# V's weights split by three engines, and dense products in the first cycle with scores

## The chip, the cores and the metric

The kernel runs on one core of one Trainium2 chip. The metric is the device time of one execution in microseconds (us). A shorter time is better.

## What is computed

The reference is a transformer block with two branches on the same normalised input, summed with the input itself. With `x` of 2048 rows and 512 columns, 32 heads of 16, all in float32:

```python
xn = layernorm(x)
# branch A: attention without a mask
q, k, v = split_heads(xn @ wqkv)            # 32 heads, 16 wide
p = softmax(q @ k.T * 16 ** -0.5)           # 2048 x 2048 for each head
A = merge_heads(p @ v) @ wo
# branch B: a gated MLP with a product over the sequence
z = gelu(xn @ w_in)                          # 2 x 896 columns
z1, z2 = z[:, :896], layernorm(z[:, 896:])
g = w_sp @ z2 + b_sp[:, None]                # 2048 x 2048 times 2048 x 896
B = (z1 * g) @ w_out
out = x + A + B
```

## The kernel before

**Arithmetic.** Every dense product (Q, K, V, both halves of `w_in`, the product over the sequence, `w_out`, `wo`) is made from operands that are split into a high and a low part of type fp32r. The helper `mm3` (lines 169 to 172) issues three matmuls for one product: high by high (L170), low by high (L171) and high by low (L172). In `v_tile` the first operand of `mm3` is the normalised and transposed `x` (`xnT`) and the second is V's weights. So L170 needs the two high parts, L171 the low part of `xnT`, and L172 the low part of the weights.

**The prologue.** Loads of `x` and of the four pieces `wv0` to `wv3` of V's weights are issued in order by SyncE. While they arrive, TensorE makes 15 matmuls on a tile of zeros (L842). A weight piece becomes a high part by a cast (L857, on GpSimd, POOL in the profile) and a low part by a subtraction in `end` (L191, on VectorE, DVE in the profile, for pieces 0 to 2, and on GpSimd for piece 3). The first two tiles of `x` are normalised (`norm_x`, statistics on DVE, L259 to L264; application on ScalarE, ACT in the profile, L268), transposed by TensorE (`turn_x`, L276), and split by `split`: the high part on ACT (L58), the low part on DVE (L167). All engines keep the order in which their instructions are written. In that order DVE makes the three low parts of the weights ahead of the low parts of `xnT`. Then follow `v_tile(0)` and `v_tile(1)`, the other two tiles of the first group of `x`, `v_tile(2)`, and so on through four groups of rows, with the first Q and K.

**The main loop.** Attention runs over 16 pairs of heads, 4 chunks of queries and 16 tiles of keys: 1024 steps. Each step has one tile of scores `st` (two matmuls, L955) whose exponential ACT takes (`exp`, tile `pf`), and, 27 steps ahead, one tile `mx` of scores (L650) of which DVE takes the largest (L658). The `st` and `mx` tiles share three pairs of PSUM banks in turn. Products of the exponentials with V (L929) gather in a PSUM bank with the tag `o`. The loop's variable `half` counts half cycles: an even one has the steps `b` and `b + 1`, an odd one the step `b + 2`, with `b = 3 * (half // 2)`. Negative ones, before the first score, only make `mx` tiles.

**Dense products in between.** A queue of generators (`qk_rest` for the remaining Q and K, then the two halves of `w_in`, the product over the sequence, `w_out`, `wo`) yields one dense product at a time. A `credit` decides how many of them follow a half cycle: 650 stands for one product of three matmuls, 512 columns each. Where `b` is negative each half cycle gets 2600, that is four. From `b = 0` on, an odd half cycle adds the share that spreads what is left over the steps up to `DENSE = 931`, and an even one gets none:

```python
if b < 0:
    credit = 2600
elif half % 2:
    credit = min(credit + 3 * (max(todo / max(DENSE - b, 10), ...
else:
    continue
```

**The accumulators of dense products.** They use the PSUM bank with the tag `d`. The group `qk_group` (four products for Q or for K of 512 rows) may also use V's bank `o` as long as no product with V is under way: while `now[0] < -2` (`now[0]` is the half cycle) its Q goes to `d` and its K to `o`. After the last product of a group, ACT copies the bank to SBUF (`qr`), behind the exponentials that stand ahead of it.

Of the kernel before, what the change touches and what calls it, by code (L numbers as in the profile page):

```python
# [10 lines left out]
AF = mybir.ActivationFunctionType  # L11
# [29 lines left out]
def fused_block(ctx, tc, x, wqkv, wo, w_in, w_spT, b_sp, w_out, out):  # L41
    nc = tc.nc
# [13 lines left out]
    def act(out, in_, func, n, **kw):  # L56
        load["A"] += 0.16 + n / 1400.0
        return nc.scalar.activation(out, in_, func, **kw)  # L58
# [48 lines left out]
    now = [-2 * LEAD // 3 - 1]  # L107
# [8 lines left out]
    def gps(us):  # L116
        pool[0] = max(pool[0], clock()) + us
        return nc.gpsimd
# [28 lines left out]
    def t512(nm):  # L147
        return big.tile([P, 512], F32, tag="t512", name=nm, bufs=4)
# [4 lines left out]
    def dpsum(nm, tag="d", n=1):  # L153
        left[0] = n
        return ps.tile([P, 512], F32, tag=tag, name=nm, bufs=1)
# [13 lines left out]
    def mm3(acc, lh, ll, rh, rl, first, last):  # L169
        nc.tensor.matmul(acc, lh, rh, start=first, stop=False)  # L170
        nc.tensor.matmul(acc, ll, rh, start=False, stop=False)  # L171
        nc.tensor.matmul(acc, lh, rl, start=False, stop=last)  # L172
# [15 lines left out]
    def end(loaded, low=None, high=False):  # L188
        t, rw, n = loaded
        if high:  # L190
            low.tensor_sub(t[:, 1, :n], rw[:, :n], t[:, 0, :n].bitcast(F32))  # L191
        elif low:
            nc.scalar.activation(t[:, 0, :n], rw[:, :n], AF.Copy)
            low.tensor_sub(t[:, 1, :n], rw[:, :n], t[:, 0, :n].bitcast(F32))
        else:
            gps(0.6).tensor_copy(t[:, 0, :n], rw[:, :n])  # L196
            gps(1.3).tensor_sub(t[:, 1, :n], rw[:, :n], t[:, 0, :n].bitcast(F32))  # L197
        return t
# [47 lines left out]
    def norm_x(g, parts=1):  # L246


        mv = sm.tile([P, 4, 2], F32, tag="mv", name=f"mv{g}", bufs=2)
        rs = sm.tile([P, 2, 4], F32, tag="rs", name=f"rs{g}", bufs=2)  # L250
        k = 4 // parts
        for a in range(parts):
            tiles = range(a * k, (a + 1) * k)
            if a:
                yield
            sl = slice(a * k, (a + 1) * k)
            for i in tiles:
                st = sm.tile([P, 6], F32, tag="bst", name=f"bst{g}_{i}", bufs=4)
                nc.vector.bn_stats(st, xs[g, i])  # L259
                nc.vector.bn_aggr(mv[:, i, :], st)  # L260
            yield
            nc.scalar.activation(rs[:, 0, sl], mv[:, sl, 1], AF.Sqrt, bias=epst)
            nc.vector.reciprocal(rs[:, 0, sl], rs[:, 0, sl])
            nc.vector.scalar_tensor_tensor(rs[:, 1, sl], mv[:, sl, 0], -1.0, rs[:, 0, sl], ALU.mult, ALU.mult)  # L264
            for i in tiles:
                if i % 4 == 2:
                    yield
                nc.scalar.activation(xs[g, i], xs[g, i], AF.Identity, bias=rs[:, 1, i:i + 1], scale=rs[:, 0, i:i + 1])  # L268
# [31 lines left out]

    def qk_group(m, g, w, tags=("d",)):
        for a in range(2):
            if now[0] < -2 and m:
                tags = ("d", "o")
            acc = dpsum(f"qk{m}_{a}_{g}", tags[a % len(tags)], ND)
            for c in range(ND):
                t = xnT[g, c]
                mm3(acc, w[a][:, 0, c * P:(c + 1) * P], w[a][:, 1, c * P:(c + 1) * P], t[:, 0, :], t[:, 1, :], c == 0, c == ND - 1)
                yield 650 + 0.5 * (c == ND - 1)
            if m == 0:  # L310
                run(qk_split(m, g, a, acc))
                yield 0
                continue
            raw_ = t512(f"qr{m}_{a}_{g}")
            act(raw_, acc, AF.Copy, 512)
            side.append(qk_split(m, g, a, raw_))
            yield 0

    def qk_split(m, g, a, src):
        hl = hilo(f"qkhl{m}_{a}_{g}")  # L320

        act(hl[:, a, :], src, AF.Copy, 512)
        yield
        if m:
            gps(1.3).tensor_sub(hl[:, 1 - a, :], src, hl[:, a, :].bitcast(F32))  # L325
            yield from pool_done()
        else:
            dve(512).tensor_sub(hl[:, 1 - a, :], src, hl[:, a, :].bitcast(F32))
        (store if m else move)((qscr, kscr)[a][m][:, :, g * 512:(g + 1) * 512], hl)
        yield  # L330
# [483 lines left out]
    def last_add(t, acc):  # L814
        f = fin[t // 2]
        dve(1024).tensor_add(f, acc, f)
        move(out[t * P:(t + 2) * P, :].rearrange("(a p) d -> p a d", p=P), f)
# [5 lines left out]
    def run(gen):  # L823
        for _ in gen:
            pass
# [9 lines left out]
    with tc.manual_schedule(engines=engines):  # L835
# [10 lines left out]
        wv = []  # L846
        for c in range(ND):
            t = (qst, kst)[c // 2][1].rearrange("p (b a f) -> p b a f", b=2, a=2)[:, c % 2]
# [4 lines left out]
        run(load_x(2))  # L853
        ones = big.tile([P, 512], F32, tag="raw", name="ones", bufs=3)
        nc.vector.memset(ones[0:32, 0:P], 1.0)
        for t, rw, n in wv:
            nc.gpsimd.tensor_copy(t[:, 0, :], rw)  # L857
        norm = norm_x(0, 2)
        next(norm)
        next(norm)  # L860
        wv = [end(l, (nc.vector, nc.gpsimd)[c == 3], True) for c, l in enumerate(wv)]
        turn_x(0, 0, 2)
        next(norm)
        nc.gpsimd.dma_start(cscr.rearrange("o (a b) -> (o a) b", b=P), ones[0:16, 0:P])
# [130 lines left out]
        for half in range(-2 * LEAD // 3, 2 * (N // 3 + 4)):  # L995
            b = 3 * (half // 2)
            ms = [b + LEAD] if half % 2 == 0 else [b + LEAD + 1, b + LEAD + 2]
            ns = [n for n in ([b, b + 1] if half % 2 == 0 else [b + 2]) if 0 <= n < N]
            now[0] = half
            flush()  # L1000
            for n in ns:
                if n == 16:
                    init_rows(1)
                if n % 64 == 14 and n // 64 + 1 < NP:
                    load_stacks(n // 64 + 1)
            pause = max(0, pause - 1.5)
            final = []
            if b + LEAD >= NSTEP and half % 2 and turn and turn[0][0] + 1 in added:
                final.append(last_mm(*turn.pop(0)))
            tiles = [(scores, n) for n in ns]  # L1010
            for i, m in enumerate(ms):
                tiles.insert(1 if half % 2 == 0 else 2 * i, (max_mm, m))
            for make, n in tiles:
                make(n)
            while ended:
                chunk_out(*ended.pop(0))
            for n in ns[:1]:
                exp(n)
            if half % 2 == 0:
                pv_some(b - 1, ready // 2 * 2)  # L1020
            for n in ns[1:]:
                exp(n)
            while behind and behind[0][0] <= half:
                nc.scalar.dma_start(*behind.pop(0)[1:])
            for f in final:
                last_add(*f)
            low = min(load.values())
            for e in load:
                load[e] = min(load[e] - low, 2.0)
            limit = load["D"] + (2.5 if half % 2 == 0 else 3.0)  # L1030
            for m in ms:
                max_red(m)

            if half % 2 == 0:
                for m in range(ms[0] - 2, ms[0] + 1):
                    max_fin(m)
            if drain:
                drain = False
                cost = next(queue[0], None)
                if cost is None:  # L1040
                    queue.pop(0)
                else:
                    pause = -cost
            bg[:] = [g for g in bg if next(g, 0) is None]
            side[:] = [g for g in side if load["D"] > limit or next(g, 0) is None]
            ready += len(ns)
            if b < 0:
                credit = 2600
            elif half % 2:
                credit = min(credit + 3 * (max(todo / max(DENSE - b, 10), 600 if b > DENSE - 15 else 0) if todo > 0 else max((todo + 64 * 650) / max(N - 6 - b, 8), 450)), 3250)  # L1050
            else:
                continue
            if urgent and between and not drain and "ones" in sel:
                queue.insert(0, urgent.pop(0))
                pause = 0
            took = 0
            while queue and not pause and not drain and go():
                cost = next(queue[0], None)
                if cost is None:
                    queue.pop(0)  # L1060
                elif cost <= 0:
                    pause = -cost
                else:
                    drain = between = cost % 1 > 0
                    credit -= cost
                    todo -= cost
                    left[0] -= 1
                    took += 1
# [38 lines left out]
```

## Time and profile before

| What | us |
|---|---|
| median of 3 runs (lowest, highest) | 1957.76 (1957.56, 1959.02) |
| the profiled execution, device time | 1960.21 |
| its span, first to last instruction | 1958.4 |
| TensorE busy in the span (matmuls) | 1938.7 |
| VectorE, ScalarE, GpSimd busy | 1373.7, 1232.5, 725.5 |
| mean granted TensorE clock | 0.997 of full |

The span is what the profile covers, and 1.8 us of the device time lie around it. The profiled execution is 2.45 us above the median of the other runs. Times in the profile's rows are counted from the start of the span. A matmul of 512 columns that follows another one starts about 0.23 us after it at the full clock, and the duration in its own row (0.39 us) includes the part in which it overlaps its neighbours.

### The profile page before, as it was taken

How to read it: one execution, taken by the hardware profiler on the slowest of the kernel's cores; microseconds unless marked ns; L12 is line 12 of the kernel's file. 1: busy time of each engine (PE TensorE's matmuls, PEld its weight loads, DVE VectorE, ACT ScalarE, POOL GpSimd, SP SyncE). 2: the span in 40 equal slices, each digit the busy share in tenths (PEclk: the TensorE clock that was granted, in tenths of full speed). 3: DMA queues.
4: the chain of work that ended last, by engine and by line, in shares of the span. 5: the costliest groups of instructions: out<-in, count | busy, mean ns of one | idle time of the engine just before them, and what ended most of it. 6: DMA issues, size and time to landing. Idle time of an engine off the chain costs nothing.

```text
span 1958.4 us, 32641 instructions
## 1 busy us (share of the span) xinstructions
PE 1938.7 (99%) x12559; PEld 1049.7 (54%) x12559; DVE 1373.7 (70%) x1565; ACT 1232.5 (63%) x1407; POOL 725.5 (37%) x790
## 2 busy tenths in 40 slices
PE   8999999999999999999999999999999999999998
PEld 7765555555555555555555555555555555555543
DVE  5356777777767677777777767777777777777872
ACT  4347778888677666656566656665666655556664
POOL 3334278889776931026122531017112400002100
PEclk9999999999999999999999999999999999999999
DMA  7566344363535535365545745346454645355323
GB/s 260 201 219 183 104 120 117 111 179 107 144 132 153 183 117 141 101 166 156 142 137 162 202 131 134 104 120 205 110 158 144 180 140 137 106 147 160 105 73 113
DMA packets 229202, 284.23 MB, mean 145 GB/s; under 512 B 35176, under 2 KB 134136, under 8 KB 226168
## 3 DMA queue, kind: packets, MB, share of 16 engines
q1 hardware_dynamic: 217240, 272.64, 47.9%
q0 software_dynamic: 2592, 8.46, 1.1%
q10 hardware_dynamic: 9216, 1.05, 0.4%
q8 instruction: 99, 1.62, 0.3%
q14 instruction: 55, 0.45, 0.1%
HBM read 188.51 MB, written 93.58 MB: 144 GB/s over the span
## 4 chain that ended last, share of the span: by engine, by line
PE 95%; DVE 2%; ACT 1%; issue 1%; DMA 0%; POOL 0%; SPq 0%; DVEq 0%; ACTq 0%
PE o L929 23%; PE mx L650 16%; PE st L955 15%; PE sp L170 7%; PE sp L172 5%; PE sp L171 5%; PE mo L170 2%; PE qk L170 2%; PE z1p L170 2%; PE z2p L170 2%; PE qk L171 1%; PE qk L172 1%; PE mo L171 1%; PE mo L172 1%; PE z1p L172 1%; PE z1p L171 1%
## 5 line engine op out<-in xcount | busy, mean ns | idle before, releaser
L658 DVE TENSOR_REDUCE mm<-mx 128x2 f32<-128x1024 f32 x1024 | 1221.9, 1222 | 498.2 <-PE mx L650 493.9
L58 ACT ACTIVATE pf<-st 128x1024 f32<-128x1024 f32 x1024 | 1028.8, 1025 | 620.0 <-PE st L955 591.6
L929 PE MATMUL o<-pf,vall 128*32 128x512 f32 (+1 forms) x5120 | 511.0, 513 | 0.0
L650 PE MATMUL mx<-kst,qst 48*128 48x512 f32 x2048 | 446.7, 434 | 2.7 <-ACT pf L58 1.8
L955 PE MATMUL st<-qst,kst 50*128 50x512 f32 x2048 | 445.2, 431 | 1.3 <-DVE mm L658 1.1
L650 PEld LDWEIGHTS mx<-kst,qst 48*128 48x128 f32 x2048 | 192.0, 185 | 268.4 <-ACT pf L58 169.6
L955 PEld LDWEIGHTS st<-qst,kst 50*128 50x128 f32 x2048 | 193.1, 185 | 164.0 <-issue 85.7
L929 PEld LDWEIGHTS o<-pf,vall 128*32 128x32 f32 x5120 | 131.4, 109 | 233.5 <-issue 211.5
L170 PE MATMUL sp<-wsp,zs 128*128 128x512 f32 x448 | 193.9, 433 | 0.3 <-DVE z1i L566 0.2
L573 POOL TENSOR_TENSOR z1i<-z1i,hhl 128x512 f32<-128x512 f32 x28 | 36.0, 1287 | 416.1 <-DVE z1i L566 413.3
L172 PE MATMUL sp<-wsp,zs 128*128 128x512 f32 x448 | 176.0, 393 | 0.0
L171 PE MATMUL sp<-wsp,zs 128*128 128x512 f32 x448 | 176.0, 393 | 0.0
L170 PEld LDWEIGHTS sp<-wsp,zs 128*128 128x128 f32 x448 | 83.9, 187 | 68.9 <-issue 51.8
L172 PEld LDWEIGHTS sp<-wsp,zs 128*128 128x128 f32 x448 | 84.1, 188 | 19.9 <-POOL wsp L197 0.5
L171 PEld LDWEIGHTS sp<-wsp,zs 128*128 128x128 f32 x448 | 84.4, 188 | 12.2
L196 POOL CAST wo<-wo0r 128x512 fp32r<-128x512 f32 x1 | 0.6, 612 | 189.6 <-DMA wo0r<-in_wo 189.6
L325 POOL TENSOR_TENSOR qkhl<-qr,qkhl 128x512 fp32r<-128x512 f32 x24 | 30.9, 1289 | 72.1 <-ACT qkhl L58 72.1
L170 PE MATMUL z2p<-w,xt 128*128 128x448 f32 x128 | 51.3, 401 | 0.0
L170 PE MATMUL mo<-wout,hp 128*128 128x512 f32 x112 | 48.5, 433 | 0.6 <-DVE xr L610 0.4
L711 POOL TENSOR_TENSOR ob<-ob 128x512 f32<-128x512 f32 (+1 forms) x16 | 20.6, 1287 | 72.8 <-DMA ob<-rscr 65.7
L172 PE MATMUL z2p<-w,xt 128*128 128x448 f32 x128 | 46.8, 366 | 0.0
L171 PE MATMUL z2p<-w,xt 128*128 128x448 f32 x128 | 46.7, 365 | 0.0
(382 smaller groups left out, 1986.3 us busy)
## 6 DMA issues: line engine op xcount, KB each, us to landing
zs<-z2scr SPq DMA_DIRECT2D x112, 512.0 KB
escr<-e SPq DMA_DIRECT2D x60, 256.0 KB
hscr<-hhl SPq DMA_DIRECT2D x28, 512.0 KB
xscr<-xnT POOLq DMA_DIRECT2D x16, 512.0 KB, 4.8
qscr<-qkhl SPq DMA_DIRECT2D x16, 512.0 KB
kscr<-qkhl SPq DMA_DIRECT2D x16, 512.0 KB
xt<-xscr SPq DMA_DIRECT2D x64, 128.0 KB
z2scr<-z2hl SPq DMA_DIRECT2D x32, 256.0 KB
```

The costliest lines, as they stand in the source:

```text
L58: return nc.scalar.activation(out, in_, func, **kw)
L170: nc.tensor.matmul(acc, lh, rh, start=first, stop=False)
L171: nc.tensor.matmul(acc, ll, rh, start=False, stop=False)
L172: nc.tensor.matmul(acc, lh, rl, start=False, stop=last)
L196: gps(0.6).tensor_copy(t[:, 0, :n], rw[:, :n])
L325: gps(1.3).tensor_sub(hl[:, 1 - a, :], src, hl[:, a, :].bitcast(F32))
L573: gps(1.3).tensor_add(z1, z1, hl[:, 1, :].bitcast(F32))
L650: nc.tensor.matmul(acc[:, j, :], qst[p % 2][rows, tt * P:(tt + 1) * P], kst[p % 2][rows, kc * 512:(kc + 1) * 512], start=True, stop=True)
L658: dve(1024).tensor_reduce(mmax[i // 16][:, :, t, kc], mstep.pop(i), AX.X, ALU.max)
L711: gps(1.3).tensor_mul(both[rows, 0, :], both[rows, 0, :], both[rows, 2, :])
L929: nc.tensor.matmul(acc[cols:cols + VW, a:a + w], vpack(kt - 1 + r, 2 * p + j), pf[:, j * 512 + a:j * 512 + a + w], start=(kt == 1 and a == ...
L955: nc.tensor.matmul(st[:, j, :], kst[p % 2][rows, kt * P:(kt + 1) * P], qst[p % 2][rows, c * 512:(c + 1) * 512], start=True, stop=True)
```

## The change

It has three parts.

1. **V's weights.** The casts of `wv0`, `wv2` and `wv3` stay on GpSimd and are written after the first part of `norm_x`. The cast of `wv1` goes to ScalarE. The subtraction for `wv2` moves from VectorE to GpSimd, which now makes those of `wv2` and `wv3`; VectorE keeps `wv0` and `wv1`.
2. **The bank of `qk_group`.** Up to half cycle 0, a group takes bank `o` if it is begun in an even half cycle and `d` in an odd one.
3. **The credit.** In the cycle `b = 0`, as long as no product with V has been made, each half cycle gets a credit of 2600, as before the first score. So the even half cycle 0 is followed by dense products too.

```diff
     def qk_group(m, g, w, tags=("d",)):
         for a in range(2):
-            if now[0] < -2 and m:
-                tags = ("d", "o")
+            if now[0] <= 0 and m:
+                tags = ("do"[now[0] % 2 == 0],)
             acc = dpsum(f"qk{m}_{a}_{g}", tags[a % len(tags)], ND)
...
-        for t, rw, n in wv:
-            nc.gpsimd.tensor_copy(t[:, 0, :], rw)
         norm = norm_x(0, 2)
         next(norm)
         next(norm)
-        wv = [end(l, (nc.vector, nc.gpsimd)[c == 3], True) for c, l in enumerate(wv)]
+        for c in (0, 2, 3):
+            nc.gpsimd.tensor_copy(wv[c][0][:, 0, :], wv[c][1])
+        nc.scalar.activation(wv[1][0][:, 0, :], wv[1][1], AF.Copy)
+        wv = [end(l, (nc.vector, nc.gpsimd)[c > 1], True) for c, l in enumerate(wv)]
         turn_x(0, 0, 2)
...
+            before = done
             for make, n in tiles:
                 make(n)
...
             ready += len(ns)
-            if b < 0:
+            if b < 0 or b == 0 and done == before:
                 credit = 2600
```

## The prediction

> **What bounds the kernel now.** I read the page first, then the table of windows, the chain of waits, and the timeline of the stretches that the table pointed to. On the page, engines' busy time and the chain that ended last:
>
> ```profile
> PE 1938.7 (99%) x12559; PEld 1049.7 (54%) x12559; DVE 1373.7 (70%) x1565; ACT 1232.5 (63%) x1407; POOL 725.5 (37%) x790
> ...
> PE 95%; DVE 2%; ACT 1%; issue 1%; DMA 0%; POOL 0%; SPq 0%; DVEq 0%; ACTq 0%
> ```
>
> TensorE (PE) sets the time, and the change removes no matmul: all 12559 stay. Only time in which PE waits, or is fed at a lower clock, can be won. The windows (length, busy time of each engine, then the granted clock) show where:
>
> ```profile
> 10.00:20.00 10.00, 8.42 (x32) 6.50 (x32) 5.44 (x13) 4.16 (x9) 7.11 (x9) 0.83 0.75 270
> 20.00:30.00 10.00, 10.00 (x53) 8.51 (x53) 5.39 (x16) 5.58 (x11) 4.09 (x8) 1.00 0.73 267
> 140.00:160.00 20.00, 19.33 (x119) 10.15 (x118) 13.89 (x17) 14.84 (x19) 3.32 (x4) 1.00 0.36 116
> 1000.00:1500.00 500.00, 499.70 (x3306) 261.95 (x3306) 360.61 (x395) 304.42 (x322) 142.39 (x135) 1.00 0.52 147
> ```
>
> PE idles 1.6 us in 10 to 20, where the clock is also below full, and 0.7 us in 140 to 160, the cycle with the first scores; the long middle has 0.3 us in 500. The chain of waits of the first 60 us (start, length, what):
>
> ```profile
> 7.51 1.10 POOL qst L857
> ...
> 9.63 1.09 DVE kst L191
> 10.72 0.34 DVE xnT L167
> 11.06 0.04 issue
> 11.11 0.50 PE v L171
> ...
> 12.73 0.43 PE v L172
> 13.16 0.43 PE v L170
> ...
> 15.72 0.23 PE v L171
> ```
>
> PE's second product with V waits for the low part of `xnT`, and that stands on DVE behind the low part of `wv2`, whose cast on POOL stands behind that of `wv1`. From 11.88 to 15.25 the products step by 0.43 us instead of 0.23 us. The timeline of the two places:
>
> ```profile
> 8.98 0.47 PE L170 MATMUL v<-qst,xnT 128*128 128x512 f32 x1 [0.56 <-ACT xnT L58]
> 10.26 1.59 POOL L191 TENSOR_TENSOR kst<-wv3r,kst 128x512 fp32r<-128x512 f32 x1
> 10.64 1.40 DVE L167 TENSOR_TENSOR xnT<-xT,xnT 128x256 fp32r<-128x256 f32 x4
> 11.11 0.50 PE L171 MATMUL v<-qst,xnT 128*128 128x512 f32 x1 [1.65 <-DVE xnT L167]
> ...
> 141.00 1.94 ACT L58 ACTIVATE pf<-st 128x1024 f32<-128x1024 f32 x2 [0.59 <-PE st L955]
> 141.01 0.40 PE L955 MATMUL st<-qst,kst 50*128 50x512 f32 x2
> 142.08 0.50 PE L650 MATMUL mx<-kst,qst 48*128 48x512 f32 x2 [0.67 <-ACT pf L58]
> 143.48 0.50 PE L170 MATMUL qk<-xnT__1212,wqk 128*128 128x512 f32 x1
> ```
>
> **The prologue, step by step.** By the landings in the trace `wv0` to `wv3` are there at 6.74, 7.46, 8.10 and 8.74 us.
>
> ACT ends the normalisation of the first two tiles at 7.38. The added cast of `wv1` (0.63, from the row of a 128x512 cast on ACT, `qkhl<-qr`) runs from 7.51 to 8.14. The next thing on ACT, the high part of `xnT`, starts at 8.45 anyway, since it waits for PE's transposes: 0.31 us of cover, so nothing. Were the cast late by more, every microsecond would go to the chain.
>
> DVE: `wv0` from 7.44 to 8.13 as now; `wv1` from 8.20, 1.07 us (its present row, next to a cast on POOL) or 0.69 (the row without a neighbour), so until 9.27 or 8.89; I take the first, because POOL casts `wv2` from 8.15. The low part of `xnT` then starts at 9.25 instead of 10.64, and PE's L171 follows 0.47 behind as now, at 9.72 instead of 11.11: **1.39 us**. Both ends: 1.0 and 1.8.
>
> Clock: the 23 products from this L171 to the end of `v_tile(1)` take 7.11 us now (11.11 to 18.22). At the full step they take 23 x 0.227 = 5.22. So the half clock costs **1.89 us**. The records give it from 11.66 to 15.07, right after a stretch of 3.41 us (8.24 to 11.66) in which PE was 35% busy, transposes counted; at the end of the kernel a stretch with 40% lost the clock too, and the lowest that kept it has 74%. With L171 at 9.72 the first stretch is 76% busy, so I expect the full clock. The Trainium skill, "TensorE: Matmul & The Clock Gate", Part 1, has the same window (3413 ns), two states, and the half rate after an idle window: the trace agrees. By that rule alone, which names no share below which a window is idle, this term is 1.89 too.
>
> POOL: now four casts and the subtraction of `wv3`, ended at 11.85. After: cast `wv0` 6.80 to 7.41; `wv2` from its landing, 8.15 to 8.76; `wv3` 8.77 to 9.84 (1.07, since DVE subtracts); subtraction of `wv2` to 11.14 and of `wv3` to 12.44 (1.29 each, as in the rows of `wqk`; 1.59 next to DVE). PE at full step reaches L172 of the third piece at 11.31, after its low part, and L172 of the fourth at 11.99, before it: **a new wait of 0.5 us** (0 to 1.2). `v_tile(1)` then ends at 12.5 + 13 x 0.227 = 15.45 instead of 18.22. Behind POOL's added work are a DMA, two memsets and the split of the first Q and K weights; they end about 0.6 us later than 17.36, and PE wants them at some 22.7: no cost. DVE and ACT normalise the next two tiles of `x` (landed 9.43 and 10.14) about 1.3 us earlier, in time for the transposes at 15.4. After that every wait up to 140 us is counted from PE, so the lead stays.
>
> Prologue: 1.39 + 1.89 - 0.5 = **2.8 us** won.
>
> **The first cycle with scores.** Its tiles start at 140.44, 140.77, 141.01, 142.08, 142.50 and 143.00, and the dense group at 143.48. Against the medians of the same steps in the middle of the kernel (0.34, 0.24, 0.23, 0.24, 0.23, 0.33) these are 1.43 us too long, because the next tiles need banks that ACT and DVE still read. The change puts a group of 12 matmuls (2.95 us by its rows) behind the third tile; ACT is then done with two exponentials at 142.94 and DVE with its maximum at 142.45, before PE comes back at 144.2: **1.43 us won**. The order of PE's instructions after the change has 339 dense stretches for 338, and by the medians of their steps the same matmuls cost 0.25 us more. Bank `o` is free again in time: its copy stands on ACT behind the third exponential, some 146.6, and the first product with V comes at 149.0. Bank `d` is not: the next group wants it at 151.0, and its copy, behind two exponentials, ends at 151.2: 0.25 us (0 to 0.5). Net **0.9 us** won.
>
> **The rest.** Six dense products made early lower the share of all later cycles by under 1%. The stages move by two or three cycles against attention. PE's steps between 250 and 530 us, where the second half of `w_in` is made and ACT has its normalisation as well, are 8.1 us longer in sum than their medians, and between 530 and 1870 us 10.5. These waits fall elsewhere after the change. I take 0, with 1 us to either side.
>
> **Sum.** 2.8 + 0.9 = 3.7 us. The profiled execution would come to 1958.4 - 3.7 = 1954.7 us of span, 1956.5 us with the 1.8 around it; it stands 2.45 above the median. From the median: 1957.76 - 3.7 = **1954.1 us**, 0.19%. About 0.2%, 3.9 us, is what a measurement of this kernel can tell from no change. The likeliest case's own range is 1952.9 to 1955.4.
>
> **Rivals.** *The timed runs had no half-clock stretch to lose.* Where the stretches of 3.41 us lie against the start of the kernel may differ between runs: placed otherwise over the same PE rows, the emptiest is 35% to 62% busy, and the trace tells only that 40% loses the clock and 74% keeps it (after the change no placing is below 65%). Then `v_tile(1)` ends at 16.33 already before, and the prologue gains 0.9, in all 1.8 us: 1955.9. For it: the profiled run, which has the stretch, is above all three others, and these spread by 1.46. The same page of the Trainium skill says that the window runs freely and that cold counts vary from run to run. Chance 0.25.
>
> *POOL becomes the bound.* If both subtractions take 1.59 and both late casts 1.1, the low part of `wv3` is ready at 13.5, PE waits 1.5 us, and 2.7 us remain: 1955.1. For it: POOL's only rows beside DVE are the long ones. Against: DVE then reads PSUM, as at 10.64, with no delay. Chance 0.11.
>
> *ACT's queue in the second half of `w_in` costs more.* There an exponential stands behind copies and normalisations, and single PE steps are up to 0.4 us late. If the shift by two cycles makes these collide more often, it decides from 3.7 us on; at double the present 8.1 us the kernel is slower by 4.4: 1962.2. Against: the numbers and sizes of ACT's instructions are the same in each cycle, only their places move. Chance 0.07.
>
> **How the numbers follow.** The forecast keeps 0.57. Its own range lies around the bound of 0.2%, with 3.7 just inside: some 0.30 of it is beyond, and a little of the other cases, 0.34 in all. Slower by over 0.2% is most of the last rival, 0.05. The rest is within, 0.61. The range reaches from 1952.3 (a full gain of 4.5 and 1 us fewer waits) to 1957.6, which takes in the first two rivals with their 1 us and some less.
>
> **What would show it.** In the profile after: L171 near 9.7; no clock below 1.00 before the end; a wait of L172 for POOL near 12; `v_tile(1)` ended near 15.4; a dense group between the third and fourth tile of the first cycle, and no wait of `mx` for `pf` there; the same 8 us between 250 and 530. It is wrong if the clock still falls, if L171 stays behind 10.5, or if the middle gains or loses over 2 us.

## The result, and the profile after

The changed kernel takes 1964.31 us (median of 8 runs, 1961.14 to 1969.68) against 1958.18 (8 runs, 1957.56 to 1961.35) for the kernel before on the same chip. The ratio is 1.0029, with a 95% interval of 1.0018 to 1.0041: it is slower by 0.29%, where 1954.1 was predicted. The changed kernel was timed again later, unaltered, beside the experiments: 1963.24 (7 runs), ratio 1.0028 (1.0017 to 1.0039).

Its profiled execution takes 1961.14 us of device time, 3.2 less than its median, where the one of before stood above its own. So the profile shows only a part of the loss. Its page, engines' busy time and the chain that ended last:

```profile
span 1959.3 us, 32635 instructions
...
PE 1938.2 (99%) x12559; PEld 1048.9 (54%) x12559; DVE 1373.7 (70%) x1566; ACT 1234.0 (63%) x1408; POOL 722.5 (37%) x786
...
PE 93%; DVE 3%; DMA 1%; ACT 1%; issue 1%; POOL 1%; SPq 0%; DVEq 0%; ACTq 0%; POOLq 0%
```

PE's work is the same; its share of the chain is 2% smaller, and DVE, DMA and POOL have taken it. The windows tell where (length, busy time of each engine, granted clock, DMA share, GB/s):

```profile
10.00:20.00 10.00, 9.23 (x43) 6.86 (x42) 5.25 (x16) 4.17 (x9) 9.83 (x13) 1.00 0.97 350
20.00:30.00 10.00, 10.00 (x54) 8.49 (x53) 4.79 (x14) 7.26 (x13) 2.79 (x7) 1.00 0.64 240
140.00:160.00 20.00, 20.00 (x121) 11.28 (x120) 13.33 (x17) 14.88 (x19) 4.45 (x4) 1.00 0.58 195
600.00:1000.00 400.00, 397.69 (x2630) 208.24 (x2622) 286.72 (x310) 248.79 (x270) 149.37 (x148) 1.00 0.52 144
1000.00:1500.00 500.00, 500.00 (x3312) 262.30 (x3308) 362.57 (x396) 304.74 (x324) 141.77 (x135) 1.00 0.52 146
```

The first three are what the change was costed for, and they came out: in 10 to 20 us the clock is full and PE idles 0.8 us instead of 1.6, in 140 to 160 it does not idle. In 600 to 1000 us PE idles 2.3 us; before, the same window had it busy for 399.97 of 400:

```profile
600.00:1000.00 400.00, 399.97 (x2636) 210.36 (x2636) 286.38 (x309) 249.53 (x272) 156.02 (x155) 1.00 0.52 145
```

No edit was made in that stretch.

The prologue, in the timeline:

```profile
7.43 0.62 ACT L861 ACTIVATE qst<-wv1r 128x512 fp32r<-128x512 f32 x1
9.08 1.42 DVE L167 TENSOR_TENSOR xnT<-xT,xnT 128x256 fp32r<-128x256 f32 x4 [0.31 <-ACT xnT L58]
9.56 0.50 PE L171 MATMUL v<-qst,xnT 128*128 128x512 f32 x1
11.12 1.28 POOL L191 TENSOR_TENSOR kst<-wv3r,kst 128x512 fp32r<-128x512 f32 x1
12.46 0.51 PE L172 MATMUL v<-kst,xnT 128*128 128x512 f32 x1 [0.29 <-POOL kst L191]
15.56 1.03 PE L276 MATMUL xT<-ident,x 128*128 128x128 f32 x8
```

L171 starts at 9.56 (predicted 9.72). L172 waits 0.29 for POOL and starts 0.68 behind the matmul ahead of it where 0.23 is usual, so the wait costs 0.45 (predicted 0.5). And `v_tile(1)` hands over to the transposes at 15.56 (15.45). The first `mx` starts 2.51 us earlier than before. Then, in the waits of PE, three lines are new or larger:

```profile
PE st L956 <- DVE mm L658: 3.1, 10, 0.5
PE mx L650 <- ACT pf L58: 2.9, 4, 1.4
PE qk L170 <- ACT vall L58: 0.3, 1, 0.3
```

The last is a cost of the bank rule that the prediction had not counted: the first K of the warm-up now begins in bank `o`, which ACT has not yet emptied of the last V tile, and the lead falls from 2.51 to 2.12 us. Before, `st` waited 1.1 us in all for DVE, and the longest wait of `mx` for ACT was 0.7.

**A ledger of the steps.** I grouped PE's instructions (a score tile, a tile of maxima, products with V, a dense stretch), took for each the time to the start of the next group, and subtracted the median of like groups between like neighbours in the profile of before. The sums in us, over score steps (excesses under 0.04 left out):

| steps (us, about) | before | after | after, 2nd profile | repay_80 | repay_190 | loan6 |
|---|---|---|---|---|---|---|
| 0 to 4 (138 to 147) | 1.43 | 0.04 | 0.04 | 0.04 | 0.04 | 0.00 |
| 4 to 40 | 0.78 | 0.54 | 0.49 | 0.53 | 0.57 | 0.76 |
| 40 to 64 (210 to 254) | 0.30 | 1.71 | 1.62 | 1.73 | 1.71 | 0.30 |
| 64 to 104 | 1.95 | 1.75 | 1.81 | 2.49 | 1.78 | 1.93 |
| 104 to 176 (325 to 456) | 4.37 | 4.74 | 4.79 | 4.40 | 4.73 | 4.36 |
| 176 to 250 | 2.05 | 2.98 | 2.94 | 2.03 | 2.92 | 2.03 |
| 250 to 330 (589 to 733) | 1.36 | 3.45 | 6.99 | 0.73 | 1.37 | 1.06 |
| 330 to 1000 | 9.45 | 9.78 | 9.47 | 8.95 | 9.30 | 9.28 |
| sum | 21.69 | 24.99 | 28.15 | 20.90 | 22.42 | 19.72 |

The last three columns are experiments, told below. After the first four steps the changed kernel loses 4.7 us more than before in its first profile (24.95 against 20.26) and 7.9 in the second. The ledger closes to within 0.5 us: its sum grows by 3.3 us in the first profile, less the lead of 2.1 that makes 1.2, and the span is 0.9 longer. For the second profile the same sum gives 4.1, and the span is 3.5 longer.

**What happens at the three places.** The change makes 18 matmuls (six products, 4.1 us at 0.227) earlier than before, beyond what the first cycle gave anyway. By the order of PE's instructions the dense work is then ahead of attention by 12 to 18 matmuls up to step 170, 12 up to 290, mostly 6 to 9 until 600, and is level at about 810. Each stage that hangs on dense work so meets other score steps. At 240 us, in the chain of waits:

```profile
237.69 0.18 DVE mrow L675
...
238.04 1.12 DVE zst L393 x2
...
239.39 2.23 DVE mm L658 x2
...
241.66 0.49 PE st L956
```

DVE's closing of a set of maxima and the statistics of the second half of `w_in` (`zst`) now stand in a row ahead of two maxima, and PE is 1.2 us late in two pieces. In the order before, these statistics came behind the same two maxima, and no wait shows there:

```profile
237.72 2.36 DVE L658 TENSOR_REDUCE mm<-mx 128x2 f32<-128x1024 f32 x2 [0.22 <-PE mx L650]
242.61 1.14 DVE L393 BATCH_NORM_STATS2 zst<-z 128x6 f32<-128x448 f32 x2
```

At 435 us, ACT has two pieces of `z2u` of that half (1.93 us) right ahead of the copy `e` and the exponentials, and PE's `mx` waits for the first of these:

```profile
433.27 1.93 ACT L58 ACTIVATE z2u<-z2u 128x896 f32<-128x896 f32 x2
435.10 0.58 ACT L58 ACTIVATE e<-o 128x512 f32<-128x512 f32 x1
435.58 1.93 ACT L58 ACTIVATE pf<-st 128x1024 f32<-128x1024 f32 x2
436.65 0.57 PE L650 MATMUL mx<-kst,qst 48*128 48x512 f32 x2 [0.99 <-ACT pf L58]
```

Before, pieces of 0.55 and 0.65 us stood there:

```profile
432.28 0.55 ACT L58 ACTIVATE z<-z2p 128x448 f32<-128x448 f32 x1
432.70 0.65 ACT L58 ACTIVATE z2hl<-z 128x512 fp32r<-128x512 f32 x1
433.22 0.61 ACT L58 ACTIVATE e<-o 128x512 f32<-128x512 f32 x1
```

The net loss at this place is small. Between 415 and 445 us PE waits 1.2 us in all in the new order (1.0 of it in this one piece), and 0.8 us in four smaller waits in the order before; the ledger's row 104 to 176, to which 435 us belongs, grows by 0.4. The row 176 to 250 (456 to 589 us) grows by 0.9 more, in small pieces, most of them before 490 us.

The largest loss is at 640 to 700 us, where the first half of `w_in` ends and `w_sp` is loaded and split. From the second profile of the changed kernel:

```profile
640.98 0.61 POOL L196 CAST wsp<-wsp_0r 128x512 fp32r<-128x512 f32 x1 [3.37 <-DMA wsp_0r<-in_w_spT]
645.20 1.30 POOL L716 TENSOR_TENSOR ohl<-ob,ohl 128x512 fp32r<-128x512 f32 x1
652.13 1.26 POOL L364 TENSOR_TENSOR z<-z 128x512 f32<-128x512 f32 x1
653.43 0.63 ACT L58 ACTIVATE z<-z 128x512 f32<-128x512 f32 x1 [3.56 <-POOL z L364]
653.96 2.91 ACT L58 ACTIVATE pf<-st 128x1024 f32<-128x1024 f32 x3
655.02 0.50 PE L650 MATMUL mx<-kst,qst 48*128 48x512 f32 x2 [2.14 <-ACT pf L58]
656.83 0.63 PE L171 MATMUL z1p<-xnT__6356,w 128*128 128x512 f32 x1
```

The same place before:

```profile
640.99 0.61 POOL L196 CAST wsp<-wsp_0r 128x512 fp32r<-128x512 f32 x1 [2.00 <-DMA wsp_0r<-in_w_spT]
648.62 1.28 POOL L364 TENSOR_TENSOR z<-z 128x512 f32<-128x512 f32 x1
651.57 0.62 ACT L58 ACTIVATE z<-z 128x512 f32<-128x512 f32 x1
```

In the new order POOL has a subtraction of attention's output stage (`ohl`, L716) and one more split of `w_sp` ahead of the last step of the gelu (L364), which ends at 653.39. The tanh of that gelu (`z`) had been written to ACT on the estimate that POOL would be done by then. It waits 3.56 us for POOL, three exponentials wait behind it, and PE's `mx`, which needs their banks, stands 2.14 us. The row after shows the second price: a matmul of 0.63 us where 0.39 is usual. The clock's records give half speed from 656.52 for 3.41 us, behind a stretch of 3.41 in which PE was busy 38%. In the first profile the tanh waited 2.87, the emptiest stretch there (652.04 to 655.46) had PE busy 56%, and the clock stayed.

### The profile page after: what moved, and what is told of

It is laid out like the page before. It is cut to its first block, busy times and chain, and to the rows that moved or that the text cites. A ratio compares the mean times of both kernels' runs of the same rounds, so it can differ in the third digit from the quotient of the medians.

```text
span 1959.3 us, 32635 instructions
## 1 busy us (share of the span) xinstructions
PE 1938.2 (99%) x12559; PEld 1048.9 (54%) x12559; DVE 1373.7 (70%) x1566; ACT 1234.0 (63%) x1408; POOL 722.5 (37%) x786
## 3 DMA queue, kind: packets, MB, share of 16 engines
q8 instruction: 99, 1.62, 0.3%
## 4 chain that ended last, share of the span: by engine, by line
PE 93%; DVE 3%; DMA 1%; ACT 1%; issue 1%; POOL 1%; SPq 0%; DVEq 0%; ACTq 0%; POOLq 0%
PE o L930 23%; PE mx L650 15%; PE st L956 15%; PE sp L170 7%; PE sp L172 5%; PE sp L171 5%; PE mo L170 2%; PE qk L170 2%; PE z2p L170 2%; DVE mm L658 2%; PE qk L171 1%; PE qk L172 1%; PE z1p L170 1%; PE mo L171 1%; PE mo L172 1%; PE z2p L172 1%
## 5 line engine op out<-in xcount | busy, mean ns | idle before, releaser
L172 PE MATMUL sp<-wsp,zs 128*128 128x512 f32 x448 | 176.2, 393 | 0.0
L171 PE MATMUL sp<-wsp,zs 128*128 128x512 f32 x448 | 175.7, 392 | 0.0
L172 PEld LDWEIGHTS sp<-wsp,zs 128*128 128x128 f32 x448 | 84.1, 188 | 19.8
L171 PEld LDWEIGHTS sp<-wsp,zs 128*128 128x128 f32 x448 | 84.4, 188 | 12.1
L172 PE MATMUL z2p<-w,xt 128*128 128x448 f32 x128 | 46.9, 366 | 0.0
L171 PE MATMUL z2p<-w,xt 128*128 128x448 f32 x128 | 46.7, 365 | 0.0
```

## Experiments

Ten runs were made, nine of other kernels and one of the changed kernel once more. Beside them the kernel before had medians of 1957.76, 1957.78 and 1957.87 (21 to 24 runs each). The theory after the result: the six products made early shift the stages against attention, and the loss is the waits at the places where they now meet. Its rivals: the loss comes from V's weights on other engines, from the bank rule and the new first cycle themselves, or from any change of the order, wherever the loan stands.

**The parts by themselves.** *p1_weights* is the kernel before with part 1 of the change alone (V's weights), *p23_credit* with parts 2 and 3 alone.

> The kernel before with part 1 alone (the weights split by three engines); the order of all matmuls and of the whole main loop is that of before. Theory A (the loss comes from the new places of the dense products in the main loop): the prologue's 2.1 to 2.5 us are kept to the end, since the main loop's order and so its waits stay: 1955.7 to 1956.1 us against 1958.2, faster by 0.11 to 0.13%. Rival B (the bank rule and the cycle with the first scores cost by themselves): the same here. Rival C (the earlier prologue itself brings the loop out of step with its transfers): the gain is lost and the kernel is slower than before by 2 us or more.

> The kernel before with parts 2 and 3 alone (bank and credit), V's weights as before. Theory A: the main loop is that of the changed kernel, so its loss of about 6 us and the 2.3 us that the prologue no longer gives: 1965 to 1968 us, slower by 0.35 to 0.5%. Rival C: no loss without part 1, some 1.2 us faster than before: 1957.

p1_weights: 1956.04 (11 runs), ratio 0.9991 (0.9983 to 1.0). p23_credit: 1964.74 (5 runs, 1960.88 to 1966.17), ratio 1.0035 (1.0022 to 1.0049), 0.3 us below the range of Theory A. So the weights bring 1.7 us in the medians, and the loss comes with parts 2 and 3, of which the first cycle was meant to bring 0.9. In the ledger, p1_weights has the 1.43 of before in steps 0 to 4 and 0.32 in 40 to 64; p23_credit has 0.04 and 1.72.

**The shift taken back at once.** *realigned* has all parts, but the cycles at once after half cycle 0 make no products until the loan is paid, and from half cycle 5 on the order is that of before:

```diff
-            if b < 0 or b == 0 and done == before:
+            if b < 0:
                 credit = 2600
+            elif half == 0:
+                owed, credit = credit, 2600
+            elif half in (1, 3):
+                credit = owed if half == 1 else credit - 2600.5
+                credit += 3 * (todo + (2600.5 if half == 1 else 1300.5)) / (DENSE - b)
+                continue
```

> All three parts, but the four products behind the half cycle 0 are a loan: half cycles 1 and 3 make none and the credit is brought to where it is before, so that from the half cycle 5 on every engine has the order of the kernel before. Theory A: prologue 2.1 to 2.5 us and the first cycle 0.8 to 1.4 us won, main loop as before: 1954.3 to 1955.3 us, faster by 0.15 to 0.2%. Rival B: the bank and the dense group in the first cycle are still there, so most of the loss of 6 us with them: 1962 or more. Rival C: slower than before too.

1959.63 (11 runs), ratio 1.0009 (1.0 to 1.0018): it misses the expected 1954.3 to 1955.3. The late places are mended (0.32 in steps 40 to 64, 1.04 in 250 to 330), but PE now stands in the first cycles, which have no dense products beside the exponentials. Its window:

```profile
140.00:160.00 20.00, 17.55 (x111) 9.30 (x110) 13.36 (x16) 14.01 (x18) 2.56 (x2) 1.00 0.39 127
```

2.45 us of idle time, where the kernel before has 0.67. Steps 0 to 40 cost 4.08 instead of 2.21. The stall was moved, not removed; the run tells that the late losses follow the order, and that a loan has to be paid back slowly.

**Another shift.** *dense934* spreads the products of the kernel before over three steps more (`DENSE = 934`), with no other edit.

> The kernel before with one number changed, DENSE 931 to 934: dense products are spread over three steps more, 0.3% fewer in each cycle, nothing else. Theory A (the waits of the main loop hang on where the dense stages fall): the sum of waits moves by several us, to the slower side if 931 is a well-placed value: 1960 to 1965. Rival B: within 1 us of before, since neither bank nor first cycle is touched.

1965.43 (5 runs), ratio 1.0039 (1.0027 to 1.0052). Slower, as Theory A said and 0.4 above its range, but mostly not at the places in question. Of its 10.3 us more in the ledger, 6.9 are in steps 760 to 931, towards the end of the dense work, with one wait of 4.3, and 1.5 are in the first four steps, where the clock is at half for 3.41 us:

```profile
PE st L955 <- DVE mm L658: 5.8, 6, 4.3
```

It shows that a small shift can open a large wait elsewhere, and tells little of the three places.

**The shift alone, and margin at one place.** *shift_later* has part 1 and neither the bank rule nor the new first cycle; three later half cycles get more credit, so that the order from about step 30 on is that of the changed kernel. *margin* is the changed kernel with two half cycles more between the gelu's work on POOL and the tanh, for the last group of the first half of `w_in` only (it is in `z1_gelu`, which the change does not touch).

```diff
# shift_later, behind the line of min(...)
+                credit += 1113 * (half in (13, 15, 17))
# margin, in z1_gelu
         yield from pool_done()
+        if g == NG - 1:
+            yield
+            yield
         act(u, u, AF.Tanh, 512, scale=GC)
```

> Part 1, but neither part 2 nor part 3: the first cycle and the banks are those of before. Instead the half cycles 13, 15 and 17 get a credit of 1113 more each, so that the dense products run ahead by about as many as in the changed kernel, and from some thirty steps on nearly every engine's order is that of the changed kernel. Theory A: the loss of the main loop is there without bank and first cycle: 1964 to 1966, slower by 0.3 to 0.4%. Rival B: as p1_weights, 1956.

> The changed kernel, with one thing altered: in the last group of rows of the first half of w_in the tanh on ScalarE is issued two half cycles later than the planner takes GpSimd to be done, seven instructions in all (about 620 to 700 us). Theory A2 (in that stage ScalarE is held in order behind GpSimd, which is held behind the transfer of w_sp, and the exponentials behind it): the steps between 250 and 330 lose most of their 2 us more than in the kernel before, and the median comes to 1961 to 1963. Rival: the time lies elsewhere, and it stays at 1964.

shift_later: 1964.58 (6 runs), ratio 1.0032 (1.0021 to 1.0044), as slow as the changed kernel: the shift makes the loss alone. Its ledger has 1.56 in steps 40 to 64, 6.78 in 250 to 330, and in its clock the half rate from 656.87 for 3.41 us again. margin: 1961.19 (11 runs), ratio 1.0016 (1.0007 to 1.0025), that is 2.1 us below *after_again* and 3.1 below the first measurement. The tanh starts at 654.40 there, without a wait. The window of 560 to 720 us in margin, and then in after_again:

```profile
560.00:720.00 160.00, 158.86 (x1046) 82.63 (x1044) 113.03 (x122) 109.01 (x129) 113.19 (x117) 1.00 0.53 152
560.00:720.00 160.00, 156.48 (x1013) 81.79 (x1012) 110.61 (x120) 106.14 (x125) 113.31 (x117) 0.99 0.54 152
```

PE idles 1.1 us there in margin and 3.5 in after_again, and the half clock is gone. So a wait of ACT for POOL is the cause of a good part at that place. It is not all of it: margin has 2.2 us of late steps between 680 and 690 us that the changed kernel does not have there (its second profile has 1.3 us just behind, at 690 to 695). They begin with a product that waits for POOL's split of `w_sp`:

```profile
683.99 0.50 PE L172 MATMUL sp<-wsp,zs 128*128 128x512 f32 x1 [0.63 <-POOL wsp L197]
```

**A slow repayment, early.** *after_again* is the changed kernel unaltered, *loan6* has part 1, puts four products behind half cycle 0 in bank `o`, and then makes 2 products in each of the odd half cycles 1 to 11 instead of 2, 2, 4, 2, 2, 4; from half cycle 13 on the order is that of before.

```diff
-            if b < 0:
+            if b < 0 or half == 0:
                 credit = 2600
+            elif half < 12 and half % 2:
+                credit = 1210.58 if half == 11 else 1300
             elif half % 2:
```

> The changed kernel, unaltered, for a second profile and more times beside the next three. Its first profile (span 1959.3 us) was its shortest run, 3 us below its median of 1964.3. Theory A: median 1963 to 1965; the profile again shows longer PE steps than before around 240, 430 and 640 to 700 us, and, if this run is a longer one, more of them where ScalarE stands behind GpSimd and GpSimd behind a transfer. A rival: the spread comes from the TensorE clock, and a longer run has stretches at half clock in the middle.

> All of part 1; of part 3 only the four dense products behind the half cycle 0, of part 2 only bank o for that group; then two products in each of the odd half cycles 1 to 11 instead of 2, 2, 4, 2, 2, 4, so that the lead of four is given back slowly and from the half cycle 13 on every engine has the order of the kernel before. Theory A: prologue as in p1_weights (1.7 us) and the first cycle's 1.43 us less some 0.4 for two more stretches: 1954.6 to 1955.4, faster by 0.12 to 0.16%. Rival B (a dense group in the first cycle and bank o cost by themselves): 1958 or more, as realigned.

after_again: 1963.24, as told above. loan6: 1955.62 (11 runs, 1954.7 to 1956.61), ratio 0.9989 (0.998 to 0.9998): the fastest version, below both kernels, and 0.2 above the range of Theory A. Its median is only 0.4 us below that of p1_weights, which the intervals do not tell apart. The stall of the first cycle is gone (0.00), and the later places are as before:

```profile
140.00:160.00 20.00, 20.00 (x134) 10.21 (x132) 14.99 (x17) 14.64 (x18) 3.86 (x3) 1.00 0.59 190
560.00:720.00 160.00, 160.00 (x1052) 83.92 (x1052) 113.48 (x125) 108.89 (x129) 115.48 (x120) 1.00 0.51 150
```

**A repayment between the places.** *repay_80* and *repay_190* are the changed kernel, whole; six cycles get less credit, the first after the place at 240 us, the second after that at 435 us as well.

```diff
# repay_80; repay_190 has range(127, 139, 2)
+                credit -= 557 * (half in range(53, 65, 2))
```

> The changed kernel, whole, but its loan is paid back by hand: six cycles from step 78 on get 557 less credit each, so that from step 100 on the dense products stand against attention as before (0 to 6 matmuls of difference, where the changed kernel has 18 at first, 12 from step 174). Theory A (the loss sits at a few places, and each needs the loan at that place): the PE excess of steps 40 to 64 (the place at 240 us) stays at 1.6 to 1.7; that of 176 to 250 falls from 2.9 to 2.1 (435 us), that of 250 to 330 from 3 to 7 to 1.0 to 1.6 (640 to 700 us). The median falls to 1957.5 to 1960. Rival B (the loss comes from the bank rule, from the first cycle or from making up any loan, and not from where the loan stands): over 1962. Rival C (cycles with fewer dense products leave PE waiting, as in the kernel named realigned): steps 64 to 104 rise from 1.8 by 1.5 or more.

> The same with the loan paid back in the six cycles from step 189 on, after the place at 435 us and before the one at 640 to 700 us. Theory A: steps 40 to 64 at 1.6 to 1.7 and 104 to 176 at 4.7 stay, the excess at 435 us stays (176 to 250: 2.5 to 3.0), and 250 to 330 falls to 1.0 to 1.6. The median is 0.5 to 1.5 us above repay_80 and 3 to 5 us below the changed kernel: 1958.5 to 1961. If the place at 640 to 700 us is not what makes the medians of the changed kernel so high, the median stays at 1962 to 1964.

repay_80: 1957.51 (11 runs), ratio 0.9999 (0.999 to 1.0008). repay_190: 1958.64 (11 runs), ratio 1.0004 (0.9995 to 1.0013). Both medians are as Theory A says. In the ledger each place stays or goes by where the loan stands when the place comes: 240 us stays in both, 435 us goes in the first alone, 640 to 700 us goes in both. (The texts above put the row 176 to 250 down to 435 us. By time 435 us lies in the row 104 to 176; the two rows go together, 4.40 and 2.03 in repay_80, 4.73 and 2.92 in repay_190.) The window of 425 to 445 us tells the two apart; repay_80:

```profile
425.00:445.00 20.00, 19.38 (x120) 10.79 (x118) 14.85 (x19) 17.12 (x22) 15.06 (x20) 1.00 0.51 144
```

and repay_190:

```profile
425.00:445.00 20.00, 18.82 (x125) 9.28 (x123) 13.99 (x19) 16.09 (x20) 18.84 (x23) 1.00 0.39 112
```

0.62 us of PE's idle time as before, and 1.18. The cost that Rival C named is seen, but smaller than it said: steps 64 to 104 rise by 0.7 in repay_80. The medians now make a ladder: 1955.62 with the loan paid back over the first cycles (loan6), 1957.51 past the place at 240 us, 1958.64 past that at 435 us, 1963.24 and 1964.31 past that at 640 to 700 us. The first step is not the price of the place at 240 us alone, since loan6 also lacks the wait at the warm-up (0.39) and the 0.7 of the repayment. The last step, 4.6 to 5.7 us, is most of the loss.

## Why the prediction failed

**The prologue: right in its parts, one term too large.** L171, the wait for POOL and the end of `v_tile(1)` came within 0.2 us, and no half clock is left in the prologue. That L171 came so close is in part luck. DVE's subtraction for `wv1` took 0.69 us, not the 1.07 of the sum, and the low part of `xnT` then waited for the high part, which came at 8.66 instead of 8.45. The gain in the two profiled executions is 2.5 us up to the first `mx` (2.8 predicted). In the medians part 1 brings 1.7.

The terms of 1.89 us for the half clock and 1.39 for L171 were made from one profiled execution, and it was an unlucky one. The profiles of p23_credit and dense934 have the same old prologue. There `wv0` landed earlier (POOL begins its cast at 5.84 and 6.02 instead of 6.80), L171 starts at 10.16 and 10.34 instead of 11.11, and there is no half clock. Their first `mx` starts at 83.86 and 84.05, before at 85.91. With the new prologue it starts between 82.61 and 83.40 in eight profiles, about 1 us earlier than in those two. In a ninth, realigned, it starts at 84.21; there DVE's subtraction for `wv1` took 1.80 us beside one on POOL. So the first rival was right in its point: the 1.7 lies between the 0.9 that it leaves for the prologue and the 2.8. Its reason is not shown. It moved the stretches of 3.41 us over the same PE rows, but here the rows themselves differ. The Trainium skill, "TensorE: Matmul & The Clock Gate", Part 1, calls the window free-running; these profiles do not test it, since in p23_credit no stretch of 3.41 us in the prologue has PE under 71% busy, wherever it is placed.

**The first cycle: right.** 1.43 us were to go, and 1.39 went (1.43 to 0.04). The bank rule cost 0.39 us at the warm-up, where the prediction had said that up to 140 us "the lead stays"; the 0.25 given for bank `d` does not show in steps 4 to 40 (0.54 against 0.78).

**The step that failed is "The rest".** It said that the waits "fall elsewhere after the change. I take 0, with 1 us to either side". Measured, they grew by 4.7 us in one profile and 7.9 in the other. From the forecast gain of 3.7 us to the loss of 5.5 to 6.1 in the medians it is 9.2 to 9.8 us. The 7.9 of the second profile, which lies nearer the median than the first, the prologue's missing 1.1 and the warm-up's 0.4 make 9.4 of it. The prediction had seen that the stages move by two or three cycles, and treated the sum of many waits as if it would average out. It does not: before, 240 us and 640 to 700 us cost next to nothing, and a shift can only add there. Nor was the price a sum of small waits of the size in the trace of before (up to 0.4 us). It came mostly from single meetings of an engine's in-order work: 1.2 us on DVE at 240 us, and 2.1 to 5.6 at 640 to 700 us with POOL, DMA and, in the second profile, the clock in a row. The 1.3 us between steps 104 and 250 are nearer to what the prediction knew: small waits, in a stretch that had such waits before.

**The third rival** ("ACT's queue in the second half of `w_in` costs more", 1962.2, chance 0.07) had the sign, and its mechanism is seen at 435 us. Its place and size were wrong: of the growth after the first cycle, 1.3 us lie in steps 104 to 250, and 2.1 to 5.6 at the change to the product over the sequence, where ACT waits for POOL. The argument against it, that "only their places move", was the reason for the loss.

**What stays open.** That the loan makes the loss is shown: shift_later has it without the bank rule and the new first cycle, and in loan6, repay_80 and repay_190 most of it is gone once the loan is paid back. The places are shown by runs that put the loan before or behind them, and at 640 to 700 us margin shows the wait behind POOL. That the two profiles differ there (3.45 and 6.99) goes with POOL's first wait for `w_sp` (1.62 us in the first, 3.37 in the second) and with the lost clock; that the DMA's arrival makes the spread is only argued. The executions of the changed kernel spread from 1961.14 to 1969.68, and no profile was taken of one above 1963.74, so what the slowest lose is not known. No run took DVE's row at 240 us or ACT's at 435 us apart by itself, and the small waits from 456 us on were not followed.

## What to carry to other kernels

An edit that moves dense work against attention must be costed at every later stage change, by setting the two orders side by side and looking at what each in-order engine then has in a row; "the waits move" is not zero where the old order has no wait. A loan of work should be paid back over several cycles before the next tight place, as loan6 does, and not all at once (realigned). Whether the loan in the first cycle then gains anything in the time beyond part 1 the medians leave open (0.4 us). An instruction that waits for another engine should be written late enough for that engine's bad days: all that stands behind it waits too.

## What the hardware showed

A gap in the middle of the kernel costs the clock earlier than expected: in after_again and shift_later a single wait of about 2 us, in a stretch of 3.41 us with PE 38% and 34% busy, brought half speed for the next 3.41 us. The Trainium skill, "TensorE: Matmul & The Clock Gate", "Why this matters for your kernels", advises against idle gaps above about 3 us; here 2.14 us was enough, so the measurement decides.

The busy share of the stretch does not settle it alone. The changed kernel kept the clock behind 56% in its first profile. But repay_190 lost it near its end, behind a stretch with PE 59% busy (1944.90 to 1948.31), and dense934 lost it in the first cycle with scores, behind 2.75 us busy of 3.41. The kernel before kept it there behind 2.74 of 3.41. First the two stretches of dense934, then that of before:

```profile
138.36:141.77 3.41, 2.75 (x15) 1.14 (x13) 2.19 (x2) 2.50 (x4) 0.03 (x1) 1.00 0.41 154
141.77:145.18 3.41, 3.41 (x10) 2.27 (x12) 1.40 (x2) 1.48 (x2) 1.28 (x1) 0.50 0.08 32
141.38:144.79 3.41, 2.74 (x14) 1.61 (x12) 3.23 (x3) 3.33 (x5) 0.57 (x1) 1.00 0.41 154
```

The stretches lost at 59% and 81% hold almost only matmuls on a part of the array (`48*128`, `50*128`, `128*32` or `32*128` in the rows), and the one kept at 80% has dense products of `128*128` from 143.48 on. That this is the reason was not tested. So the prediction's reading, that a share of 74% keeps the clock, held for its stretch but is no rule.
